# Attention with a top-1 mixture of experts: a reordered start, two steps of VectorE moved, and the experts' tokens turned by half-row transposes

## The chip, the cores and the metric

The kernel runs on one core of a Trainium2 chip. The metric is the device time of one execution in microseconds. The engines are TensorE (PE in the rows; PEld is its weight load), VectorE (DVE), ScalarE (ACT), GpSimd (POOL) and SyncE (SP). DMAs are issued from the queues of SP, ScalarE and GpSimd.

## The reference

```python
def _attn_ref(q, k, v, s):                      # (8, 8, 576, 64); s is (8, 8, 576)
    scores = scale * np.matmul(q, k.transpose(0, 1, 3, 2))
    cum = np.cumsum(np.maximum(s, 0.0), axis=-1)
    bias = -(cum[:, :, :, None] - cum[:, :, None, :])
    scores = np.where(causal, -1000000000.0, scores + np.minimum(bias, 0.0))
    attn = softmax(scores)
    return np.matmul(attn, v)

def _moe_ref(x, w_gate, w1, w2):                # x: (4608, 512), 8 experts, hidden 1024
    probs = softmax(x @ w_gate); expert_idx = argmax(probs)
    for e in range(E):
        out[mask_e] = gate_w * (np.maximum(xe @ w1[e], 0.0) @ w2[e])
```

Each token goes to the one expert with the highest logit.

## The kernel before, in words

**Attention.** The 64 heads are worked in 32 pairs, two heads on 128 partitions. For a pair, the scores of five query groups (S0 to S4) are TensorE products in fp32r; q and k are split into a high and a low part, and three products of the parts are summed. The decay bias enters as one more product: a selector `pick` times a table `cu`, built once at the start from the running sum of s. VectorE takes the row maximum while it evicts the scores (Z), ScalarE the exponentials (X), TensorE turns them by 64-row transposes (T, `half_turn`, L294), VectorE or ScalarE evicts them (C), TensorE multiplies with v (AV), and VectorE copies the output (XB). GpSimd makes the low parts of q and k for the next pairs (L215, L222).

The start (`__init__`, L77 to L174) is outside that order: VectorE clips s (L138), takes the running sum (L139), the centres (L141, L144) and the low part (L147), makes the low parts of pair 0 (`split`, L215 and L222), and then builds the table group by group (`build`, L184), after ScalarE has centred each group (`center`, L177). While nothing else is ready TensorE runs a warm-up of products of zeros (L157 to L162).

**The order.** For attention each engine has a list, written out by hand, of steps with a lag in pairs (`ORDER`, L37 to L42); `loop` emits them in turn as their needs are met. Each four pairs make a batch of tokens, whose routing (RA to RD, with CH1, CH2, CI, EX, EI, DI and SE between) is threaded through the same lists. Step 0 makes the logits, step 1 turns them and takes their maximum (`route`, L381 to L420), step 2 ranks the tokens (L421 to L445, with the operation on `base` at L439), steps 3 to 7 turn and scale the tokens (L446 to L458). `scale` (L343 to L355) takes the reciprocals of the softmax sums; SE calls it for the last batch but one. GpSimd then scatters token rows to the buffer `xs` in DRAM (L465). `HASTE` places the steps of the last batch but one by hand; the last batch is routed inside expert 0's first layer.

**Experts.** For each expert, `load_x` and `finish_x` bring 512 rows and a tail from `xs` into `xr`. The tokens must stand with their 512 features on partitions: `trans_group` (L786 to L795) turns one group of 128 features by four TensorE transposes of 128x128 into one PSUM bank of the pool `ps_x` (three banks), and `split` (L729) evicts it into a high part on ScalarE (L730) and a low part on VectorE (L731). `layer1` (L811) runs 96 products of 512 columns (L820), `layer2` (L858) 24 products for each of four token blocks (L846). The transposes for the next expert stand between those blocks (`run`, L982 to L987):

```python
for k in range(NSTAT):
    self.layer2(e, k)
    for d in ((0, 1), (2,), (3,), ())[k] if more else ():
        self.trans_group(e + 1, d)
    if more and k == (1 if e else X0[1]):
        x4 = self.trans_block(...)
```

`trans_block` turns the fifth block of rows by four more whole transposes (L800). What is left of the tokens is worked by `tails` in branches that depend on the counts.

Of the kernel before, what the change touches and what calls it, by code (L numbers as in the profile page):

```python
# [8 lines left out]
F32 = mybir.dt.float32  # L9
# [35 lines left out]
WARM = 24  # L45
# [6 lines left out]
THIN_AT = (2, 2)  # L52
X0 = (1, 2, 1)
# [23 lines left out]
class Attention:  # L77
    def __init__(self, ctx, tc, K, qkv, s, rt, ps_t):
# [39 lines left out]
        nc.gpsimd.memset(self.half, 0.0)  # L118
        for h in range(2):
            nc.gpsimd.memset(self.half[64 * h : 64 * h + 64, h], 1.0)  # L120
# [3 lines left out]
        nc.gpsimd.memset(self.mask8, 0.0)  # L124
# [4 lines left out]
        for h in range(2):  # L129
            r = slice(64 * h, 64 * h + 64)  # L130
            nc.gpsimd.affine_select(
                out=self.mask8[r, 512:], in_=self.mask8[r, 512:], pattern=[[-1, 64]],
                compare_op=ALU.is_ge, fill=BIG, base=0, channel_multiplier=1,
            )
        self.split(0, 5)
        for part in (0, 2):
            self.split(0, part)
# [19 lines left out]
        for x in range(WARM):  # L157
            for c in ((0, 256), (256, 512)) if x % 3 == 0 else ((0, 512),):
                nc.tensor.matmul(
                    warm[:, c[0] : c[1]], zb[:, :P], zb[:, P + c[0] : P + c[1]],  # L160
                    start=True, stop=True, skip_group_check=True,
                )  # L162
        nc.gpsimd.memset(self.Es[MIX][:, S:], 0.0)
        self.LT = rt.tile([P, 640], F32, name="LT", bufs=1)
        nc.gpsimd.memset(self.LT[:, S:], 0.0)
        self.xb, self.sums, self.sumx, self.rr, self.ra = [], [], [], [], []
        for i in range(2):
            self.xb.append(rt.tile([P, 4, 640], F32, name=f"xb{i}", bufs=1))
            nc.gpsimd.memset(self.xb[i][:, :, S:], 0.0)
            self.sums.append(rt.tile([P, 4, 8], F32, name=f"sums{i}", bufs=1))  # L170
            self.sumx.append(rt.tile([P, 4], F32, name=f"sumx{i}", bufs=1))
            self.rr.append(rt.tile([P, 5, 8], F32, name=f"rr{i}", bufs=1))
            nc.gpsimd.memset(self.rr[i][:, 4], 1.0)
            self.ra.append(rt.tile([P, 2, 5, 4], F32, name=f"ra{i}", bufs=1))  # L174

    def center(self, g):
        self.nc.scalar.activation(  # L177
            self.cu[:, TO[g] : TO[g] + TW[g]], self.cum[:, : TW[g]], AF.Identity,
            scale=self.sign[:, 0:1], bias=self.cen[:, 0, g : g + 1],
        )  # L180
# [25 lines left out]
    def split(self, p, part):  # L206
# [3 lines left out]
        if part == 0:  # L210
            d["q"] = self.lq.tile([P, 2, S], F32R, name="q")
            nc.scalar.activation(d["q"][:, 0], q, AF.Copy)  # L212
# [3 lines left out]
        elif part == 2:  # L216
            d["kh"] = self.ld.tile([P, S], F32R, name="kh")
            nc.scalar.activation(d["kh"], k, AF.Copy)
# [399 lines left out]
    def loop(self):  # L618
# [6 lines left out]
        self.todo = constants(self.nc, self.const, self.K, self.wg)  # L625
# [73 lines left out]
class Experts:  # L699
# [86 lines left out]
    def trans_group(self, e, d):  # L786
# [7 lines left out]
        self.split(x[:, 0, d], x[:, 1, d], t)  # L794

# [169 lines left out]
    def run(self):  # L965
        for e in range(E):
# [24 lines left out]
def constants(nc, cp, K, wg):  # L991
    blank = cp.tile([P, WIDE], F32, name="blank")[:, :ROW]
    nc.gpsimd.memset(blank[:, : DM + 1], 0.0)
    nc.gpsimd.iota(blank[:, DM + 1 :].bitcast(I32), pattern=[[0, 1]], base=1 << 20, channel_multiplier=0)
    K["blank"] = blank
    K["wg"] = cp.tile([P, 4, 32], F32, name="wg")
# [115 lines left out]
```

## Time and profile before

| | |
|---|---|
| median of the three runs shown | 785.6 us (785.55, 785.6, 787.28) |
| the profiled execution | 784.42 us, of which the span is 782.7 us |
| busy TensorE | 758.6 us (97% of the span) |
| busy VectorE, ScalarE, GpSimd | 477.2, 414.7, 219.6 us |
| attention, then experts | about 0 to 322 us, then to the end |

A row gives the start, the time taken, the engine, the line of the kernel, the operation, what it writes and reads, its shape and how many were merged; what stands in brackets is how long the engine sat idle before it, and what ended that.

### The profile page before, as it was taken

The page shows a single profiled execution, that of the slowest core. Times are in us where ns is not written, and L with a number is a line of the kernel's source. Part 1 is how long each engine was busy: PE and PEld are TensorE (multiplying, and loading weights), DVE is VectorE, ACT ScalarE, POOL GpSimd, SP SyncE. Part 2 cuts the span into 40 slices and gives each one's busy share as a digit, 9 for nine tenths or more (in the row PEclk, how much of TensorE's full clock was granted, in tenths as well). Part 3 has the DMA queues.
Part 4 walks back from the last instruction along what each step waited for, and adds up shares of the span by engine and source line. Part 5 has one row for each costly group of instructions (what it writes and reads, how often), then busy time and mean ns, then how long its engine had stood idle before and what let it go on. Part 6 is the DMA issues. An engine that isn't in the chain of part 4 may idle for free.

```text
span 782.7 us, 17835 instructions
## 1 busy us (share of the span) xinstructions
PE 758.6 (97%) x6972; PEld 624.4 (80%) x6972; DVE 477.2 (61%) x1247; ACT 414.7 (53%) x1002; POOL 219.6 (28%) x328
## 2 busy tenths in 40 slices
PE   7999999999999988999999999999999999999995
PEld 5888888888888867678788887888888888888874
DVE  7778989899999999655263544522642453633520
ACT  7998888888888866523251432412521431513410
POOL 7544455656564645321001011010011001010011
PEclk9999999999999999999999999999999999999998
DMA  7763234434343414575172642710630271720101
GB/s 263 220 217 99 96 123 131 137 116 150 103 151 107 163 53 149 189 242 201 49 249 95 212 153 87 273 44 16 218 134 28 97 259 57 255 95 22 54 29 41
DMA packets 43903, 105.24 MB, mean 134 GB/s; under 512 B 3983, under 2 KB 3983, under 8 KB 43792
## 3 DMA queue, kind: packets, MB, share of 16 engines
q1 hardware_dynamic: 35408, 80.13, 30.6%
q0 software_dynamic: 5936, 18.92, 6.5%
q10 hardware_dynamic: 2448, 4.74, 1.8%
q8 instruction: 67, 1.10, 0.6%
q14 instruction: 44, 0.36, 0.2%
HBM read 75.91 MB, written 28.12 MB: 133 GB/s over the span
## 4 chain that ended last, share of the span: by engine, by line
issue 37%; DMA 12%; PE 4%; another core or an unknown queue 4%; POOL 3%; DVE 2%; POOLq 1%; ACT 1%; DVEq 0%
DMA xs<-xr,dsi 6%; DMA out_dram<-y,xr 6%; POOL out_dram L853 2%; PE t L332 1%; PE ph L820 1%; PE s L238 1%; PE t L296 0%; DVE z L278 0%; ACT aT L322 0%; POOLq L946 0%; DVE dd L406 0%; POOLq L853 0%; DVE xb L321 0%; POOLq L1107 0%
## 5 line engine op out<-in xcount | busy, mean ns | idle before, releaser
L846 PE MATMUL py<-w2t,hT 128*128 128x512 f32 x768 | 181.3, 392 | 1.2 <-DVEq L960 1.2
L820 PE MATMUL ph<-xT,w1t 128*128 128x512 f32 x768 | 178.3, 391 | 0.6 <-PEq L949 0.6
L820 PEld LDWEIGHTS ph<-xT,w1t 128*128 128x128 f32 x768 | 143.2, 188 | 31.9 <-issue 2.3
L292 ACT ACTIVATE E<-z,m 128x128 f32<-128x128 f32 (+4 forms) x288 | 165.8, 580 | 3.1 <-DVE m L278 3.1
L846 PEld LDWEIGHTS py<-w2t,hT 128*128 128x128 f32 x768 | 142.6, 188 | 30.4 <-issue 1.5
L853 POOL DMA_INDIRECT out_dram<-y,xr x39 | 37.9, 972 | 393.6 <-DVE y L852 331.0
L278 DVE CUSTOM_DVE_ANT_0 z<-s,mask 128x128 f32<-128x128 f32 (+4 forms) x288 | 139.0, 516 | 6.4 <-ACT E L292 0.6
L852 DVE TENSOR_SCALAR y<-py,xr 128x512 f32<-128x512 f32 x35 | 26.3, 751 | 117.5 <-PE py L846 117.5
L332 PE MATMUL t<-aT,v 128*64 128x64 f32 (+2 forms) x1408 | 95.2, 291 | 0.1
L822 ACT ACTIVATE hT<-ph 128x512 fp32r<-128x512 f32 x64 | 38.1, 596 | 96.4 <-PE ph L820 96.0
L332 PEld LDWEIGHTS t<-aT,v 128*64 128x64 f32 x1408 | 66.6, 137 | 18.8 <-issue 2.8
L825 DVE SCALAR_TENSOR_TENSOR hT<-ph,hT 128x512 fp32r<-128x512 f32 x64 | 44.2, 690 | 60.7 <-ACT hT L822 60.6
L238 PE MATMUL s<-kh,q 64*128 64x512 f32 (+3 forms) x512 | 80.2, 318 | 0.0
L322 ACT COPY aT<-t 128x1024 f32<-128x1024 f32 x64 | 57.5, 898 | 38.0 <-PE t L296 38.0
L238 PE MATMUL s<-cu,pick 64*128 64x128 f32 (+4 forms) x320 | 71.9, 374 | 2.5 <-DVE base L439 1.2
L296 PEld LDWEIGHTS t<-ident,E 64*128 64x128 f32 x1600 | 63.8, 138 | 9.2 <-ACT E L292 2.7
L296 PE MATMUL t<-ident,E 64*128 64x64 f32 x1600 | 67.4, 223 | 2.4 <-ACT E L292 0.9
L730 ACT ACTIVATE xT<-t 128x512 fp32r<-128x512 f32 x32 | 18.4, 597 | 90.9 <-PE t L793 90.9
L321 DVE COPY aT<-t 128x256 f32<-128x256 f32 (+2 forms) x96 | 61.6, 641 | 3.9 <-PE t L296 3.5
L292 ACT ACTIVATION_READ_ACCUMULATOR E<-z,m 128x1 f32 x288 | 55.3, 192 | 0.0
L238 PEld LDWEIGHTS s<-cu,pick 64*128 64x128 f32 (+1 forms) x320 | 36.6, 186 | 22.3 <-issue 10.1
L215 POOL TENSOR_TENSOR q<-qk,q 128x576 fp32r<-128x576 f32 x31 | 44.2, 1426 | 32.1 <-ACT q L212 32.0
(159 smaller groups left out, 1016.6 us busy)
## 6 DMA issues: line engine op xcount, KB each, us to landing
raw<-in_w_dram SPq DMA_DIRECT2D x32, 1024.0 KB, 5.8
qk<-in_qkv_dram SPq DMA_DIRECT2D x32, 576.0 KB, 3.9
v<-in_qkv_dram SPq DMA_DIRECT2D x32, 320.0 KB, 4.3
xr<-xs SPq DMA_DIRECT2D x8, 1028.0 KB, 5.7
xs<-blank ACTq DMA_DIRECT2D x9, 514.0 KB, 5.8
xs<-blank SPq DMA_DIRECT2D x8, 514.0 KB, 4.3
xr<-xs SPq DMA_DIRECT2D x8, 514.0 KB, 8.6
xs<-xr,dsi POOLq DMA_INDIRECT x40, 3.4
```

Of the source, the lines that this page charges most:

```text
L215: return e.tensor_tensor(out=d["q"][:, 1], in0=q, in1=d["q"][:, 0].bitcast(F32), op=ALU.subtract)
L238: self.nc.tensor.matmul(out, terms[n][0], terms[n][1], start=n == 0, stop=n == len(terms) - 1, skip_group_check=True)
L278: ins = nc.vector.tensor_tensor_reduce(out=cut(z[:, :w]), in0=x, in1=mask, scale=-0.125, scalar=3.0e38, op0=ALU.add, op1=ALU.min, accum_out=m,
L292: nc.scalar.activation(out, z[:, :w], AF.Exp, bias=m, scale=-1.0, accum_out=total)
L296: self.nc.tensor.transpose(out, src[r], self.K["ident"][r, r])
L321: return self.nc.vector.tensor_copy(o, i)
L322: return self.nc.scalar.copy(o, i)
L332: nc.tensor.matmul(ps[64 * h : 64 * h + 64, bank, lo - 512 * bank : hi - 512 * bank], v[:, kt, h], self.aT[p % 2][:, kt, h, lo:hi], start= ...
L820: nc.tensor.matmul(ps, w[:, a, d, c], x[:, b, d], start=n == 0, stop=n == 11)
L825: nc.vector.scalar_tensor_tensor(out=h[:, 1, f], in0=ps, scalar=0.0, in1=h[:, 0, f].bitcast(F32), op0=ALU.max, op1=ALU.subtract)
L846: self.nc.tensor.matmul(ps, hT[:, a, f, c], w[:, b, f % 4], start=f == 0 and i == 0, stop=f == 7 and i == 2)
L853: disjoint(self.tc, "out", self.nc.gpsimd.indirect_dma_start(out=self.out, out_offset=IndirectOffsetOnAxis(ap=row[:, DM + 1 : DM + 2].bitc ...
```

## The change

At the start: s comes in two loads of 64 rows, on two queues, instead of four of 32; q and k of pair 0 come as two loads on the same two queues; the first centre and the first build go ahead of the splits of pair 0; the `half` memsets and the selector of pair 0 go ahead on GpSimd, and the memsets of `mask8`, of the fifth score tile's pad and of `blank` wait for VectorE's last split of pair 0; the pads of the logits and of the output buffers move into the generator of constants, whose steps VectorE's CO calls, so that the later constants and the load of the gate weights come one pair later. The warm-up has 12 rounds of four products with 128 columns and 6 of one with 512, instead of 24 rounds of 512 columns in one or two products. In VectorE's order SE moves from the end of a round (lag 3) to behind RDd (lag 4, so to the next round), and CI from behind RCd to ahead of Z2. The tokens of experts 1 to 7 are turned by transposes of 64 rows, in two runs of sixteen (two groups of 128 features, four token blocks, two row halves that lie in two PSUM banks), one behind layer 2's first block and one behind its third. The kernel's text in short:

```diff
-    "DVE": "RAd+4 RDd+4 C4+3 ... RBd+3 Z2+2 RCd+3 CI+3 C1+2 XB+3 Z0+1 CO+1 SE+3",
+    "DVE": "RAd+4 RDd+4 SE+4 C4+3 ... RBd+3 CI+3 Z2+2 RCd+3 C1+2 XB+3 Z0+1 CO+1",
-WARM = 24
+WARM = 18
+PAIR_AT = (0, 2)
...
+        nc.gpsimd.memset(self.half, 0.0)
+        for h in range(2):
+            nc.gpsimd.memset(self.half[64 * h : 64 * h + 64, h], 1.0)
         s4 = s.rearrange("(p h) c -> h p c", h=2)
-        for x in range(4):
-            nc.sync.dma_start(raw[32 * x : 32 * x + 32], s4[x // 2])
-        self.load(0)
+        x = self.ldx.tile([P, 2 * S], F32, name="qk")
+        for i, queue in enumerate((nc.sync, nc.scalar)):
+            queue.dma_start(raw[64 * i : 64 * i + 64], s4[i].unsqueeze(0).broadcast_to([2, 32, S]))
+        for i, queue in enumerate((nc.sync, nc.scalar)):
+            queue.dma_start(x[:, S * i : S * i + S], self.qkv[0][:, S * i : S * i + S])
+        self.st[0] = dict(x=x)
+        self.split(0, 5)
...
-        self.split(0, 5)
-        for part in (0, 2):
-            self.split(0, part)
...
-        for g in ORD:
+        self.center(ORD[0])
+        for part in (0, 2):
+            keep(self.split(0, part))
+        for g in ORD[1:]:
             self.center(g)
         keep(nc.vector.tensor_scalar(out=low, ...))
+        self.build(ORD[0])
         for part in (1, 3):
-            keep(self.split(0, part))
-        self.build(ORD[0])
+            ins = self.split(0, part)
+            keep(ins)
+        self.begun = getattr(ins, "ins", ins).name
+        after(tc, nc.gpsimd.memset(self.mask8, 0.0), [self.begun])
...
         for x in range(WARM):
-            for c in ((0, 256), (256, 512)) if x % 3 == 0 else ((0, 512),):
+            w = P if x < 12 else 512
+            for c in range(0, 512, w):
                 nc.tensor.matmul(
-                    warm[:, c[0] : c[1]], zb[:, :P], zb[:, P + c[0] : P + c[1]],
+                    warm[:, c : c + w], zb[:, :P], zb[:, P + c : P + c + w], start=True, stop=True, skip_group_check=True
...
+    def blanks(self):
+        nc = self.nc
+        rest = constants(self.tc, self.const, self.K, self.wg, self.begun)
+        yield next(rest)
+        nc.gpsimd.memset(self.LT[:, S:], 0.0)
+        for i in range(2):
+            nc.gpsimd.memset(self.xb[i][:, :, S:], 0.0)
+            nc.gpsimd.memset(self.rr[i][:, 4], 1.0)
+        yield
+        yield from rest
...
+    def trans_pair(self, e, i):
+        xr = self.X[e][0]
+        if i == 0:
+            self.X[e][1] = self.xt.tile([P, 2, 4, 512], F32R, name="xT")
+        x = self.X[e][1]
+        ts = [self.turned() for a in range(2)]
+        for d in range(2):
+            for k in range(NSTAT):
+                for a in range(2):
+                    r = slice(HP * a, HP * a + HP)
+                    o = HP * (NSTAT * d + k)
+                    c = P * (2 * i + d)
+                    self.nc.tensor.transpose(ts[a][:, o : o + HP], xr[r, k, c : c + P], self.K["ident"][r, r])
+        for a in range(2):
+            hi, lo = (
+                x[:, b, 2 * i : 2 * i + 2].rearrange("p d (k a c) -> p a d k c", k=NSTAT, a=2)[:, a] for b in range(2)
+            )
+            self.split(hi, lo, ts[a].rearrange("p (d k c) -> p d k c", d=2, k=NSTAT))
...
-                for d in ((0, 1), (2,), (3,), ())[k] if more else ():
-                    self.trans_group(e + 1, d)
+                if more and k in PAIR_AT:
+                    self.trans_pair(e + 1, PAIR_AT.index(k))
```

## Rows read from the trace of the kernel before

**Rows 1.** Busy time by stretch: PE, PEld, DVE, ACT, POOL, then granted clock, DMA share, GB/s

```profile
0.00:20.00 20.00, 15.75 (x143) 10.77 (x145) 15.96 (x43) 14.54 (x33) 15.58 (x49) 1.00 0.76 265
...
100.00:200.00 100.00, 100.00 (x1613) 84.02 (x1610) 90.94 (x302) 85.91 (x239) 56.09 (x81) 1.00 0.41 136
...
700.00:750.00 50.00, 49.88 (x234) 40.77 (x232) 20.25 (x33) 18.07 (x34) 2.87 (x3) 1.00 0.11 36
```

**Rows 2.** Timeline of the start up to the first scores, from several engines

```profile
0.82 1.79 SPq L109 DMA_DIRECT2D aT<-in_s_dram  x4
...
4.32 0.46 DVE L138 TENSOR_SCALAR aT<-aT 128x576 f32<-128x576 f32 x1 [1.75 <-DMA aT<-in_s_dram]
...
4.91 1.46 POOL L231 TENSOR_TENSOR pick<-sel,half 128x128 fp32r<-128x128 f32 x1
...
6.50 0.68 ACT L212 ACTIVATE q<-qk 128x576 fp32r<-128x576 f32 x1 [3.67 <-DMA qk<-in_qkv_dram]
...
8.56 1.56 DVE L184 SCALAR_TENSOR_TENSOR cu<-aT,cen,cu 128x128 fp32r<-128x128 f32 x3
...
9.09 0.33 PE L238 MATMUL s<-cu,pick 64*128 64x128 f32 x2 [0.18 <-POOL pick L230]
```

**Rows 3.** Timeline near 12 us: a build on VectorE beside a split on GpSimd

```profile
11.93 1.41 POOL L215 TENSOR_TENSOR q<-qk,q 128x576 fp32r<-128x576 f32 x1 [1.16 <-ACT q L212]
...
11.99 1.76 DVE L184 SCALAR_TENSOR_TENSOR cu<-aT,cen,cu 128x384 fp32r<-128x384 f32 x1
```

**Rows 4.** Timeline of the warm-up: its products, and its last 19 weight loads

```profile
1.60 7.31 PE L159 MATMUL s<-aT 128*128 128x256 bf16 x32 [1.60 <-DVE aT L103]
...
5.42 3.00 PEld L159 LDWEIGHTS <-aT 128*128 128x128 bf16 x19 [0.28 <-issue]
```

**Rows 5.** Timeline of the scale step of batch 6 and what waits for it

```profile
280.64 1.41 POOL L215 TENSOR_TENSOR q<-qk,q 128x576 fp32r<-128x576 f32 x1
...
281.07 1.01 DVE L351 TENSOR_SCALAR rr<-sums 128x32 f32<-128x32 f32 x1
...
284.25 0.16 DVE L439 TENSOR_TENSOR base<-base,s 128x8 f32<-128x8 f32 x1
...
284.56 0.38 PE L238 MATMUL s<-cu,pick 64*128 64x256 f32 x2 [1.22 <-DVE base L439]
```

**Rows 6.** Timeline of the logits' maximum of batch 6; last, all eight of L406 (min/median/max)

```profile
291.56 0.32 DVE L397 TENSOR_TENSOR both<-part 128x160 f32<-128x160 f32 x1
...
292.25 1.44 POOL L215 TENSOR_TENSOR q<-qk,q 128x576 fp32r<-128x576 f32 x1
...
292.62 2.50 DVE L406 TENSOR_TENSOR dd<-L,mx 128x40 f32<-128x40 f32 x1
...
293.62 1.42 POOL L222 TENSOR_TENSOR kl<-qk,kh 128x576 fp32r<-128x576 f32 x1
...
296.85 0.46 PE L296 MATMUL s<-ident,xb 64*128 64x64 f32 x8 [2.39 <-DVE m L278]
...
L406 DVE TENSOR_TENSOR dd<-L,mx x8: 190/200/2497, 78.7 to 333.3; 128x40 f32<-128x40 f32 x8
```

**Rows 7.** Timeline of PE: products around eight whole transposes, and a layer of 96

```profile
412.19 0.62 PE L846 MATMUL py<-w2t,hT 128*128 128x512 f32 x2
...
413.75 0.63 PE L846 MATMUL py<-w2t,hT 128*128 128x512 f32 x2
...
431.56 22.02 PE L820 MATMUL ph<-xT,w1t 128*128 128x512 f32 x96 [0.15 <-PEq L949]
```

**Rows 8.** Timeline of PE and PEld: products around sixteen half transposes of the routing

```profile
336.97 0.40 PE L820 MATMUL ph<-xT,w1t 128*128 128x512 f32 x1
...
337.30 0.57 PEld L296 LDWEIGHTS t<-ident,xb 64*128 64x128 f32 x16 [0.37 <-DVE num L1064]
...
338.29 0.39 PE L820 MATMUL ph<-xT,w1t 128*128 128x512 f32 x1
```

**Rows 9.** Groups by line and shape: weight loads of half transposes

```profile
L296 PEld LDWEIGHTS t<-ident,E 64*128 64x128 f32 x1600 | 63.8, 138 | 9.2 <-ACT E L292 2.7 <-issue 1.3 <-ACT aT L322 0.4
```

More of the change, by code (lines that the diff above doesn't have):

```diff
@@ L117, in __init__ @@
             nc.gpsimd.memset(sign[32 * x : 32 * x + 32, 1:2], 8.0 * (x % 2))
-        nc.gpsimd.memset(self.half, 0.0)
-        for h in range(2):
-            nc.gpsimd.memset(self.half[64 * h : 64 * h + 64, h], 1.0)
         self.mask = cp.tile([P, 640], F32, name="mask")
@@ L128, in __init__ @@
         )
[L129 to L134, printed above, removed]
-        self.split(0, 5)
-        for part in (0, 2):
-            self.split(0, part)
         keep(nc.vector.tensor_scalar(out=raw, in0=raw, scalar1=0.0, scalar2=None, op0=ALU.max))
@@ L144, in __init__ @@
         keep(nc.vector.tensor_scalar(out=self.cen[:, 1], in0=mid, scalar1=sign[:, 1:2], scalar2=None, op0=ALU.mult))
-        for g in ORD:
+        self.center(ORD[0])
+        for part in (0, 2):
+            keep(self.split(0, part))
+        for g in ORD[1:]:
             self.center(g)
         keep(nc.vector.tensor_scalar(out=low, in0=cum, scalar1=sign[:, 1:2], scalar2=None, op0=ALU.mult))
+        self.build(ORD[0])
         for part in (1, 3):
-            keep(self.split(0, part))
-        self.build(ORD[0])
+            ins = self.split(0, part)
+            keep(ins)
+        self.begun = getattr(ins, "ins", ins).name
+        after(tc, nc.gpsimd.memset(self.mask8, 0.0), [self.begun])
+        for h in range(2):
+            r = slice(64 * h, 64 * h + 64)
+            nc.gpsimd.affine_select(
+                out=self.mask8[r, 512:], in_=self.mask8[r, 512:], pattern=[[-1, 64]],
+                compare_op=ALU.is_ge, fill=BIG, base=0, channel_multiplier=1,
+            )
         self.build(ORD[1])
@@ L157, in __init__ @@
         for x in range(WARM):
-            for c in ((0, 256), (256, 512)) if x % 3 == 0 else ((0, 512),):
+            w = P if x < 12 else 512
+            for c in range(0, 512, w):
                 nc.tensor.matmul(
-                    warm[:, c[0] : c[1]], zb[:, :P], zb[:, P + c[0] : P + c[1]],
-                    start=True, stop=True, skip_group_check=True,
+                    warm[:, c : c + w], zb[:, :P], zb[:, P + c : P + c + w], start=True, stop=True, skip_group_check=True
                 )
-        nc.gpsimd.memset(self.Es[MIX][:, S:], 0.0)
+        after(tc, nc.gpsimd.memset(self.Es[MIX][:, S:], 0.0), [self.begun])
         self.LT = rt.tile([P, 640], F32, name="LT", bufs=1)
-        nc.gpsimd.memset(self.LT[:, S:], 0.0)
         self.xb, self.sums, self.sumx, self.rr, self.ra = [], [], [], [], []
@@ L624, in loop @@
         self.plan()
[L625 removed]
+        self.todo = self.blanks()
         self.unbuilt = list(ORD[3:])
@@ L989, in run, with constants @@
                 self.tails(e, x4)
-def constants(nc, cp, K, wg):
+def constants(tc, cp, K, wg, begun):
+    nc = tc.nc
     blank = cp.tile([P, WIDE], F32, name="blank")[:, :ROW]
-    nc.gpsimd.memset(blank[:, : DM + 1], 0.0)
+    after(tc, nc.gpsimd.memset(blank[:, : DM + 1], 0.0), [begun])
     nc.gpsimd.iota(blank[:, DM + 1 :].bitcast(I32), pattern=[[0, 1]], base=1 << 20, channel_multiplier=0)
     K["blank"] = blank
+    yield
     K["wg"] = cp.tile([P, 4, 32], F32, name="wg")
```

13 lines of the change are left out of this document (6 added, 7 removed), and 2 rows, old and new, of the table ORDER.

## The prediction

> **What bounds the kernel now.** I read the busy time by stretch first, because one share for the whole span would hide the stages. From 100 to 200 us TensorE is busy all the time, and from 700 to 750 us it idles 0.12 us [rows 1]: attention in its steady state and the experts are both bound by TensorE. The granted clock is 1.00 in these stretches and in the first 20 us, the 2.4 GHz level [rows 1]. So time is to be had in two ways only: fewer TensorE nanoseconds in the experts, or fewer holes where TensorE is not yet bound (the first 20 us) or is held up (280 to 300 us, at the end of attention). Then the timeline of those two stretches: at the start one chain of VectorE, fed by loads and by ScalarE, leads to the first scores at 9.09 us [rows 2]; at the end two waits of TensorE stand out, 1.22 us and 2.39 us, both released by VectorE [rows 5, 6]. Last the timeline of TensorE around the transposes, to price a run of them as it lies between long products [rows 7, 8].
>
> **Part 1, the start.** VectorE idles until the four loads of the gate input s have landed, at 4.32 us; their four issues on SP take 1.79 us [rows 2], 0.45 us each, and the last one decides. Now two issues on two queues do it, each with 64 rows, so the last starts 1.3 us earlier; I count 1.0 us, because a load is twice as large. From there the chain runs without a gap: clip, running sum, centres, low part, two splits of q and k, first build, first scores [rows 2]. In the new order the first centre and the first build go ahead of the splits, which shortens nothing in sum (VectorE does the same work ahead of the second build), but the splits must not become late: ScalarE's split of q waited for qk until 6.50 [rows 2]. qk is now issued in two halves right behind s, on both queues, about 1.2 us earlier, so it comes earlier by as much as the chain does. The mask memsets, the two pads and the blank go behind the start of the splits on GpSimd; they are about 2.5 us of its time, hidden by its waits for ScalarE's q (1.16 us at 11.93 [rows 3]); if that cover were gone, GpSimd's split for pair 1 would hold the scores of pair 1 back. I take a gain of 1.0 us. Bounds: nothing, if GpSimd's pick product (1.46 us in the trace [rows 2]) now falls before the signs that the centres read; and 2.2 us, if also the build of 1.76 us is no longer held by the GpSimd split that starts 0.06 us before it [rows 3] (three builds ahead of it took 1.56 us together [rows 2], so up to 1.2 us is in that); the two could as well start in the other order, but nothing in the trace says so.
>
> **Part 2, the warm-up.** 9216 columns instead of 12288, 48 of the 54 products with 128. In the trace the products run at half pace until about 5.4 us, though the granted clock reads 1.00 there too: 13 of 32 are out by then, in 3.8 us, and the other 19, 7424 columns, take 3.5 us [rows 4]. So 128 columns cost about 0.105 us before that point and half of that after it: 36 small products to 5.4 us, 12 more in 0.7 us, and six of 512 in 1.4 us: the end is near 7.5 us, where it was 8.91, and the last split is then due at about 7.9. It costs nothing, hidden by the chain of part 1; if the chain gained more than 1.5 us, the warm-up would be next.
>
> **Part 3, the turn to the experts.** Two steps of VectorE's hand-written order move. Scale of batch 6 (SE) now stands behind the rank step instead of ahead of it. In the trace its small operations start at 281.07 and drag, the first for 1.01 us, beside the GpSimd split that began at 280.64; only at 284.25 comes the base operation that frees the score bank, and TensorE waits 1.22 us for it [rows 5]. With the two rank operations first, base is done near 281.5, before TensorE asks. The drag stays, as GpSimd sets its end, but VectorE's next eviction starts 0.3 us sooner and the row maximum behind it need not wait another 0.3 us for its scores: by VectorE, which is late next, 0.65 us remain of the 1.22. The second: the logits' maximum (CI) goes ahead of a pair of row maxima and one scaled block. In the trace its last operation, 128x40 elements, takes 2.50 us: it begins at 292.62, after a GpSimd split began, and ends when the next one ends (293.62 plus 1.42); the median of its eight is 0.2 us. Behind it queue an eviction, the output copy and the row maximum for which TensorE waits 2.39 us [rows 6]. Moved ahead, the four operations end 1.2 us after the logits, near 291.2, before the GpSimd split that starts at 292.25. What they push back: the pair of row maxima by 1.2 us, which frees a score bank that TensorE asks for only after its products with v, and ScalarE's exponentials, which stand behind the late operation anyway. VectorE then reaches the row maximum after the scores of pair 31 with TensorE some 0.5 us ahead: about 1.8 us of the 2.39 are gained. Both together 2.45 us; bounds 0.65 (the second gains nothing) and 3.6 (both waits vanish).
>
> **Part 4, the transposes of experts 1 to 7.** Each expert had 16 whole transposes, and now 32 of half the rows, in two runs of 16. What a run costs is what it adds between long products. One product of 512 columns takes 0.228 us (22.02 us for 96). Two products before a run of 8 whole transposes start at 412.19, the second product behind it at 413.75: 1.56 less three products is 0.877 us, 0.110 each [rows 7]. For halves the route steps inside expert 0's first layer show the same form: last product before at 336.97, second product behind at 338.29: 1.32 less two products is 0.865 us for 16 halves [rows 8]. The 16 weight loads themselves fill 0.57 us, so that 0.3 us of each run are entry and exit: the loads begin 0.10 us after the product before has streamed, and the product behind comes late. Per expert: 16 x 0.110 = 1.75 us before, 2 x 0.865 = 1.73 after, 0.02 us gained, 0.15 us over seven. The evictions stay 4 and 4 of 512 elements per expert, written in pieces of 64; they lie beside the next 24 products (5.5 us) and cost nothing; two banks at once of three are free there. Bounds: a gain of 0.3 us per run if entry and exit vanished (4.1 us more in all), a loss as in the fourth rival. The nearest row is the run itself, so I take 0.15.
> The Trainium skill speaks on both sides here. TensorEngine Tiling (Array Packing), Theoretical Speedup, gives up to 2x for a small dimension of 64; by that, as an estimate, this part would be 6.1 us instead of 0.15 (half of 1.75, seven times); rival (a) is its case. Its Key Properties say that changing the tiling mode drains the engine; the 0.3 us of [rows 8] agree with that one.
>
> **Sum.** 1.0 + 2.45 + 0.15 = 3.6 us off the profiled execution's 784.42, which lies 0.15% under the median of the runs, 785.6. As a median: 782.0. Nothing behind 300 us gives it back: TensorE is bound again from there, the waits for loads that the trace shows there are ScalarE's and not TensorE's, and the tail of the last store is as before.
>
> **Rivals.** (a) The drain is hidden in this place and halves run as fast as their loads: two runs of about 0.57 us [rows 8], 0.6 us less per expert, 4.1 us more: 777.9. For it: loads fill their run without a hole. Against: [rows 8]. (b) The second move of part 3 puts a new wait in place of the one removed: the row maxima 1.2 us later hold the exponentials, and TensorE its transposes, for as long; of part 3 only 0.65 stays: 783.8, within 0.3%. For it: VectorE and ScalarE are both near full in attention (91 and 86 of 100 us [rows 1]). (c) The start gains nothing, as k now comes over ScalarE's queue and GpSimd works behind: 783.0. (d) Slower: the two row halves don't run side by side. One weight load of a half takes 138 ns [rows 9]; one after the other, 32 of them are 4.4 us where 1.75 stood, plus 0.6 of entry and exit: 3.3 us x 7 = 23 us, 805. It decides from about 62 ns for a half, entry and exit apart (0.84 us more per expert: 2.4 us and the 3.45 of the other parts, over seven). Against it: 16 loads in 0.57 us [rows 8]. The Trainium skill's TensorE: Matmul & The Clock Gate (LDWEIGHTS) gives a load the same time whatever its rows; the 138 ns agree, and taken alone it would speak for (d). (e) The change doesn't do what it says at the start: with small products the clock still stands at 1.2 GHz at the first scores. TensorE's 15.75 us of work up to 20 us [rows 1], less the warm-up's 7.31 [rows 4], would take up to twice that, of which waits hide half: 4 us lost and 1.0 not gained: 787.
>
> **How the numbers follow.** The three runs shown lie 0.22% apart, so 0.3%, 2.4 us, is about what a measurement can tell from no change. Forecast 0.56, (a) 0.12, (b) 0.16, (c) 0.09, (d) 0.03, (e) 0.04. Faster: 0.56 less a twentieth for its own slow end, (a) and (c), which lies 2.6 us under the median: 0.74. Same: (b) and that twentieth: 0.19. Slower: (d) and (e): 0.07. The range takes in the forecast, (b) and (c), and half the way to (a), by part 1's upper bound too: 778.8 to 784.4.
>
> **What would show it.** First scores at about 8 us; the base operation before 282 and no wait of 1.2 us behind it; the 128x40 operation at 0.2 us and TensorE's 2.39 us wait under 0.6; a run of 16 halves between products at 0.87 us and an expert's period, product to product, unchanged within 0.1 us. Wrong would be: periods shorter by 0.5 us or more, which is (a), a new VectorE wait between 290 and 300 us, which is (b), or first scores at 9 us or later.

## The result, and the profile after

The changed kernel takes 792.05 us (median; 791.25 to 792.75, four runs) against 785.95 us: a ratio of 1.0078 [1.0061, 1.0096]. It is slower by 0.8%, where 3.6 us less were forecast. The profiled execution took 792.75 us, with a span of 791.0 us. Medians leave out two executions far slower than the others of their kernel: one of 804.92 us of the kernel before, on the third chip used below, and one of 1482.04 us of the version with 65 warm-up products.

The first thing to read is where the two traces part. This table gives the start of the same product in each (us), and the distance to the kernel before:

| TensorE begins | before | after | distance |
|---|---|---|---|
| first scores | 9.09 | 17.31 | +8.2 |
| first product with v | 23.63 | 33.41 | +9.8 |
| a product with v late in attention | 276.58 | 286.51 | +9.9 |
| the same, next batch (SE lies between) | 290.63 | 299.06 | +8.4 |
| the same, one more (CI lies between) | 304.18 | 310.68 | +6.5 |
| expert 1, first layer | 385.44 | 391.47 | +6.0 |
| expert 7, first layer | 715.23 | 723.34 | +8.1 |
| span | 782.7 | 791.0 | +8.3 |

So nearly 10 us are lost ahead of the first product with v, the two moved steps give back 3.4 us of them, and 2 us are lost again among the experts. The timeline of the start of the changed kernel, which answers to [rows 2] and [rows 4]:

```profile
0.81 0.74 SPq L114 DMA_DIRECT2D aT<-in_s_dram  x1
0.81 1.45 ACTq L114 DMA_DIRECT2D aT<-in_s_dram  x1
...
1.60 7.01 PE L167 MATMUL s<-aT 128*128 128x128 bf16 x54 [1.60 <-DVE aT L104]
...
13.95 0.46 DVE L133 TENSOR_SCALAR aT<-aT 128x576 f32<-128x576 f32 x1 [12.05 <-DMA aT<-in_s_dram]
...
16.17 0.49 ACT L192 ACTIVATE cu<-aT,cen,sign 128x128 fp32r<-128x128 f32 x1 [11.46 <-DVE cen L136]
...
17.31 0.47 PE L253 MATMUL s<-cu,pick 64*128 64x128 f32 x2 [8.71 <-DVE cu L199]
```

VectorE's clip of s starts at 13.95 us instead of 4.32: it waits 12.05 us for a load that was issued at 0.81. Both issues are over by 2.3 us, so it is the transfer itself that is long. What a transfer lacks is seen in the DMA view of the first 20 us of the same kernel (40 slices of half a microsecond; the first line is the mean busy share of the 16 DMA engines in tenths, the last two give KB each):

```profile
DMA  0000037899999999999999831111138899821105
GB/s 0 0 0 0 9 88 152 237 287 296 284 286 313 286 249 295 263 257 276 326 328 291 260 113 57 48 55 46 55 68 141 345 400 403 183 72 51 44 16 132
...
aT<-in_s_dram SPq DMA_DIRECT2D x1, 144.0 KB
aT<-in_s_dram ACTq DMA_DIRECT2D x1, 144.0 KB
```

From 12 to 14.5 us the digits are 1, at some 50 GB/s: most of the sixteen engines have nothing left to do, and some two of them (a tenth to two tenths of sixteen) still carry the loads of s. Total bandwidth is not what they wait for. The times at which the semaphores of the loads count up, which the trace holds too, say the same. The first load of s in the kernel before counts up in sixteen steps, from 2.46 to 2.75 us. Each of the two wide loads has one step soon after its issue and two late ones: at 9.17 and 9.97 us on SP's queue, at 13.27 and 13.92 on ScalarE's. VectorE starts 0.03 us after the last of them.

The late start costs a second time. The busy time by stretch (TensorE, its weight loads, VectorE, ScalarE, GpSimd, then granted clock, DMA share, GB/s) of the changed kernel:

```profile
5.00:10.00 5.00, 3.60 (x24) 2.32 (x22) 0.00 (x0) 0.00 (x0) 0.00 (x0) 1.00 1.04 283
10.00:15.00 5.00, 0.00 (x0) 0.00 (x0) 1.02 (x2) 0.00 (x0) 0.00 (x0) 0.60 0.43 132
15.00:20.00 5.00, 2.19 (x14) 1.85 (x16) 4.66 (x12) 3.83 (x7) 1.79 (x5) 0.50 0.57 179
20.00:25.00 5.00, 5.00 (x28) 3.86 (x26) 3.84 (x15) 4.78 (x15) 4.73 (x9) 0.53 0.33 108
```

TensorE is idle from 8.6 to 17.3 us, the granted clock falls to 0.50 (1.2 GHz) in that idle time, and nearly all scores up to 25 us are computed at that level. That is the step from +8.2 to +9.8 in the table; with the loads cut (below), which keeps the clock at 1.00, the same two rows lie 1.24 and 1.21 us ahead, without such a step. In the kernel before the clock was 1.00 here [rows 1].

At the turn to the experts, the timeline of VectorE in the changed kernel answers to [rows 5]:

```profile
290.88 0.16 DVE L454 TENSOR_TENSOR base<-base,s 128x8 f32<-128x8 f32 x1
290.96 0.61 DVE L366 TENSOR_SCALAR rr<-sums 128x32 f32<-128x32 f32 x1
291.49 1.46 DVE L366 TENSOR_SCALAR rr<-sumx 64x4 f32<-64x4 f32 x2
```

The view of one source line answers to the last row of [rows 6] (ns, min/median/max):

```profile
L421 DVE TENSOR_TENSOR dd<-L,mx x8: 190/200/202, 88.7 to 339.8; 128x40 f32<-128x40 f32 x8
```

The base operation comes ahead of the scale's small ones, which still drag (1.46 us for two), but TensorE no longer waits for them; and none of the eight 128x40 operations takes 2.50 us any more. Of TensorE's two waits the one of 1.22 us is gone, and of the 2.39 us 0.45 are left:

```profile
303.34 0.46 PE L311 MATMUL s<-ident,xb 64*128 64x64 f32 x8 [0.45 <-DVE m L293]
```

### The profile page after: what moved, and what is told of

It is laid out like the page before. It is cut to its first block, busy times and chain, and to the rows that moved or that the text cites. A ratio compares the mean times of both kernels' runs of the same rounds, so it can differ in the third digit from the quotient of the medians.

```text
span 791.0 us, 18096 instructions
## 1 busy us (share of the span) xinstructions
PE 761.3 (96%) x7106; PEld 624.3 (79%) x7106; DVE 473.2 (60%) x1247; ACT 414.7 (52%) x1002; POOL 218.5 (28%) x328
## 4 chain that ended last, share of the span: by engine, by line
PE 37%; issue 37%; DMA 14%; another core or an unknown queue 4%; POOL 3%; DVE 2%; ACT 1%; POOLq 1%; ACTq 0%; DVEq 0%
PE s L253 16%; PE t L347 12%; DMA xs<-xr,dsi 6%; DMA out_dram<-y,xr 6%; PE t L311 6%; POOL out_dram L887 2%; DMA qk<-in_qkv_dram 2%; PE s L311 2%; PE ph L854 1%; PE s L390 1%; ACT E L307 1%; ACT aT L337 1%; DVE z L293 0%; DVE rr L366 0%
## 5 line engine op out<-in xcount | busy, mean ns | idle before, releaser
L253 PEld LDWEIGHTS s<-kh,q 64*128 64x128 f32 x512 | 50.2, 189 | 1.6 <-ACT kh L233 0.3
```

Of the source, the lines that this page charges most:

```text
L253: self.nc.tensor.matmul(out, terms[n][0], terms[n][1], start=n == 0, stop=n == len(terms) - 1, skip_group_check=True)
```

## Experiments

Two theories for the start were set against each other. Theory 1: the shape of the load is at fault. Each load of s is now described as 2 by 32 rows (the 2 is the repeat), and few engines carry a load whose outer count is 2. Theory 2: the queues or the new order of the loads are at fault. Twelve kernels were compared with the kernel before on the same chip; four more settled what was then open. The kernel before took 785.58 us on the chip of the first four, 791.2 to 792.0 us on the chips of the others, so times are compared as ratios on one chip. The one trace of the kernel before has the first chip's time, 784.42 us; of the sixteen runs the first four were traced there, the others on the other three chips.

**Cut loads.** The changed kernel, each 64-row load as two of 32 rows, same queue:

```diff
-            queue.dma_start(raw[64 * i : 64 * i + 64], s4[i].unsqueeze(0).broadcast_to([2, 32, S]))
+            for j in range(2):
+                queue.dma_start(raw[64 * i + 32 * j : 64 * i + 32 * j + 32], s4[i])
```

> The changed kernel, but each of the two 64-row loads of s is cut into two loads of 32 rows on the same queue, so that nothing differs but how the same bytes are cut. Theory 1 (a load whose outermost dimension is 2 is carried by two of the sixteen DMA engines only, so s lands 10 us late and all that is queued on those two engines behind it): s lands by 4 us, first scores near 8 us, granted clock 1.00 throughout, and the time is before less 1.0 (start), 3.4 (order) and 0.4 (transposes): about 781, between 780 and 782.5. Theory 2 (two queues at once hold each other up, ScalarE's above all): s still lands later than 10 us, the time stays at 791 to 793.

Measured: 781.73 us against 785.58, ratio 0.9961 [0.9948, 0.9973]. Its timeline:

```profile
3.95 0.46 DVE L134 TENSOR_SCALAR aT<-aT 128x576 f32<-128x576 f32 x1 [2.06 <-DMA aT<-in_s_dram]
...
7.85 0.33 PE L254 MATMUL s<-cu,pick 64*128 64x128 f32 x2
```

This one edit takes the 10 us away: theory 1, not the queues, and not the order. The first scores now come 1.24 us ahead of [rows 2], but the loads are not what gives that: the clip starts 0.37 us earlier (3.95 for 4.32). By the first transposes the lead is down to 0.33 us (11.96 for 12.29), and it is 1.21 us at the first product with v (22.42 for 23.63). In between stands the last build of the table, 1.76 us long beside GpSimd's split in [rows 3]; here the split begins at 12.67 us, behind it:

```profile
11.59 0.61 DVE L200 SCALAR_TENSOR_TENSOR cu<-aT,cen,cu 128x384 fp32r<-128x384 f32 x1
```

**Wide loads alone.** The kernel before, its four loads of s as two 64-row loads, both on SP:

```diff
-        for x in range(4):
-            nc.sync.dma_start(raw[32 * x : 32 * x + 32], s4[x // 2])
+        for i in range(2):
+            nc.sync.dma_start(raw[64 * i : 64 * i + 64], s4[i].unsqueeze(0).broadcast_to([2, 32, S]))
```

> The kernel before, with s in two loads of 64 rows, both on SP, in place of four of 32; nothing else. Theory 1: s lands at 8 us or later (64 packets for each of two engines), q and k behind it, first scores between 13 and 18 us, time 7 to 11 us over before, 792 to 797. Theory 2: one queue, so nothing changes: first scores at 9 us, time 785 to 787.

Measured: 798.39 us, ratio 1.0165 [1.0147, 1.0182]; more than expected. Its timeline and its stretches:

```profile
13.62 0.46 DVE L138 TENSOR_SCALAR aT<-aT 128x576 f32<-128x576 f32 x1 [11.04 <-DMA aT<-in_s_dram]
```

```profile
15.00:20.00 5.00, 0.00 (x0) 0.00 (x0) 3.99 (x7) 4.04 (x8) 2.84 (x5) 0.50 0.48 150
20.00:25.00 5.00, 4.30 (x28) 3.52 (x28) 4.73 (x13) 3.08 (x10) 2.46 (x3) 0.50 0.52 182
```

The cause alone, on one queue and in the old order, reproduces the wait, and the low clock with it. It is dearer here by some 3 us (the first product with v is 12.5 us late, for 9.8): with q and k behind the loads on the same queue, ScalarE's split of q, too, starts at 14.70 us, and the first scores at 20.26 us.

**Repeat or count?** A load of 2 by 32 rows has a small outer count and also reads each row twice. The first try to part the two described the first load of q and k as 2 by 64 rows:

```diff
-        self.nc.sync.dma_start(x, self.qkv[p][:, : 2 * S])
+        src = self.qkv[p][:, : 2 * S]
+        self.nc.sync.dma_start(x, src.rearrange("(a p) c -> a p c", a=2) if p == 0 else src)
```

> The kernel before with one edit: the first load of q and k (128 rows, 590 KB) is described as two parts of 64 rows, without any repeated source; the same bytes, the same queue, one issue. If what made the loads of s slow is that their outermost count is 2, this load becomes slow too: with s in two parts 295 KB took some 11 us, so 590 KB take 20 us or more, ScalarE's split of q starts behind 20 us where it started at 6.50, and the time is 12 us or more over the kernel before. If it was that each source row was read twice, the split starts at 6.5 us as before and the time is the same.

It tested nothing: the two halves lie one behind the other in memory, and the built program holds the load merged into 128 rows, as before (790.71 us, the kernel before beside it 791.23). So its trace shows the kernel before on the second chip. With `"(p a) c -> a p c"` in the same place, even rows and then odd rows, it can't be merged, and a = 16 is the control (the first pair then has its rows in another order, so these two kernels don't compute the reference):

> The kernel before with one edit: the first load of q and k (128 rows, 590 KB, SP's queue) reads its rows in another order, all even ones and then all odd ones, so that the source is described as 2 by 64 rows and cannot be merged into one row count; each row is read once, and the bytes are the same. It changes the values of the first pair. If a count of 2 on the outside of a load is what makes it slow, ScalarE's split of q, which started at 6.50 us in the kernel before, starts behind 20 us, since 295 KB of s in two such parts took some 11 us. If it was the reading of each row twice, it starts at 6.5 us as before.

> The same edit with 16 by 8 rows (each sixteenth row together), again every row once and the same bytes; it changes the values of the first pair. If the count on the outside decides, 16 is as good as 128: ScalarE's split of q starts at 6.5 us within 0.5. If any order of rows that cannot be merged makes a load slow, it starts as late as with 2 by 64.

ScalarE's split of q, which stands at 6.50 in [rows 2], with a = 2 and with a = 16 (802.32 and 793.08 us, one run each, beside 791.4):

```profile
18.26 0.68 ACT L213 ACTIVATE q<-qk 128x576 fp32r<-128x576 f32 x1 [15.43 <-DMA qk<-in_qkv_dram]
```

```profile
7.73 0.68 ACT L213 ACTIVATE q<-qk 128x576 fp32r<-128x576 f32 x1 [4.89 <-DMA qk<-in_qkv_dram]
```

Each row is read once in both, and the bytes are the same: an outer count of 2 delays the load by 11.8 us, one of 16 by 1.2 (more than the half microsecond allowed). The count decides, not the repeat. The Trainium skill's page DMA: Bandwidth & Descriptors, section Why a DMA increments its semaphore by 16 and not by 1, has the rule: a transfer is spread over the largest number of engines up to 16 that divides the slowest dimension of both sides. By it the changed loads get two engines; the digit 1 in the DMA view agrees, and so do the semaphores: two late steps for each wide load of s and for this load with a = 2 (18.03 and 18.24 us), sixteen steps with a = 16 (7.04 to 7.71 us).

**The two moved steps alone.** The kernel before with only VectorE's new order:

```diff
-    "DVE": "RAd+4 RDd+4 C4+3 Z1+2 Z3+2 C0+2 Z4+2 SC+4 DI+4 CH2+4 CH1+4 RBd+3 Z2+2 RCd+3 CI+3 C1+2 XB+3 Z0+1 CO+1 SE+3",
+    "DVE": "RAd+4 RDd+4 SE+4 C4+3 Z1+2 Z3+2 C0+2 Z4+2 SC+4 DI+4 CH2+4 CH1+4 RBd+3 CI+3 Z2+2 RCd+3 C1+2 XB+3 Z0+1 CO+1",
```

> The kernel before with SE and CI moved in VectorE's order, nothing else. Theory: both waits of TensorE go, as in the changed kernel, where the distance to before fell by 1.5 us over the scale step and by 1.9 us over the logits' maximum: 3.4 us faster, 782.3 to 783.0. Rival: a part of that came from the later start (another phase of GpSimd against VectorE): only the predicted 2.45 or less, 783.5 or more.

Measured: 780.83 us, ratio 0.9945 [0.993, 0.9959]. By the ratio that is 4.3 us and by the medians 4.75, more than expected. Its trace shows less than that: against the kernel before, the product with v is 1.3 us earlier behind SE (289.30 for 290.63) and 3.25 behind CI (300.93 for 304.18); the spans differ by 3.9 (778.8 for 782.7), as expert 0 lacks a hole of 0.61 us that the kernel before has. For the rest, another run with the kernel before's order gives a hint.

**The half transposes alone.** The kernel before with the transposes of experts 1 to 7 in row halves:

```diff
-                for d in ((0, 1), (2,), (3,), ())[k] if more else ():
-                    self.trans_group(e + 1, d)
+                if more and k in PAIR_AT:
+                    self.trans_pair(e + 1, PAIR_AT.index(k))
```

> The kernel before with the tokens of experts 1 to 7 turned by half-row transposes, nothing else. Theory (entry and exit of a run cost what the halves save): between 0 and 0.6 us faster in all, a run of 16 between products at 0.87 us. Rival (a): 4 us faster. Rival (d) and its kin: slower by 1 us or more; the changed kernel's distance grew by 0.8 us at one tail and 1.7 us at one layer, and if the new transposes cause that, it shows here again at the same places.

Measured: 784.03 us, ratio 0.998 [0.9969, 0.999]. Its stretches around the end of attention, which it shares with the kernel before, and below them those of the run with the moved steps alone:

```profile
295.00:300.00 5.00, 2.91 (x48) 2.67 (x50) 4.80 (x14) 3.34 (x11) 3.70 (x6) 0.87 0.68 235
300.00:305.00 5.00, 4.53 (x51) 3.79 (x47) 3.31 (x14) 3.95 (x11) 0.00 (x0) 0.79 0.31 109
```

```profile
295.00:300.00 5.00, 4.54 (x63) 3.81 (x59) 4.69 (x18) 5.00 (x15) 2.47 (x3) 1.00 0.92 333
300.00:305.00 5.00, 4.46 (x82) 3.61 (x84) 4.06 (x17) 1.53 (x6) 2.91 (x3) 1.00 0.29 112
```

Behind TensorE's 2.39 us wait the granted clock can fall to 1.2 GHz. Here it did, and the distance to the kernel before's trace grew from 0.25 to 1.74 us across that place. In the profiled execution of before it happened not to. Among the 21 runs of the kernel before beside it the two with the highest mean clock (0.997) took 783.9 us and the two with the lowest (0.991, 0.992) 786.2 and 786.8; the five runs with the moved steps all have 0.996 or 0.997. So on this chip removing the wait also removes the chance of low clock behind it; that this is what is missing is likely, not shown.

On the three other chips it is otherwise, against what was expected of the runs there: in all seven traces that have the moved steps VectorE holds TensorE anew, for 1.4 to 2.2 us at 298 to 300 us, and between 300 and 315 us the clock falls to 0.50 to 0.69 of a stretch. What holds VectorE there no view names. One of them, with 32 warm-up products (below):

```profile
299.82 0.45 PE L254 MATMUL s<-cu,pick 64*128 64x384 f32 x2 [2.17 <-DVE m L294]
...
300.00:305.00 5.00, 4.41 (x51) 3.73 (x52) 4.75 (x21) 2.88 (x9) 1.54 (x2) 0.52 0.08 32
```

As to the transposes: before and after, one second layer of 96 products (first row of each, and the first product of the layer behind it, which stands at 431.56 in [rows 7]):

```profile
407.20 5.61 PE L846 MATMUL py<-w2t,hT 128*128 128x512 f32 x24
412.64 1.04 PE L793 MATMUL t<-ident,xr 128*128 128x128 f32 x8
413.43 5.72 PE L846 MATMUL py<-w2t,hT 128*128 128x512 f32 x24
```

```profile
413.23 5.60 PE L880 MATMUL py<-w2t,hT 128*128 128x512 f32 x24
418.76 0.71 PE L823 MATMUL t<-ident,xr 64*128 64x64 f32 x16
419.41 5.75 PE L880 MATMUL py<-w2t,hT 128*128 128x512 f32 x24
...
437.55 2.75 PE L854 MATMUL ph<-xT,w1t 128*128 128x512 f32 x11
```

The layer takes 24.36 us before (431.56 less 407.20) and 24.32 after (437.55 less 413.23): 0.04 us for this expert. A run of 16 halves holds TensorE 0.65 us where 8 whole ones held it 0.79, but it starts later: product to product over it is 6.18 us (419.41 less 413.23), over the whole ones 6.23 (413.43 less 407.20). The growth of 0.8 and 1.7 us that the changed kernel shows at one tail and at one layer is not there in the run with the transposes alone (-0.04 and +0.17 us), so they don't cause it.

**The start and the steps in pairs.** What the parts are worth together, on one other chip:

> The kernel before with the new start alone (order of the loads, splits, builds and memsets, and the warm-up with small products), but each 64-row load of s cut into two loads of 32 rows; VectorE's order and the transposes as before. Theory 1 (the parts add up): first scores near 7.9 us, attention 1.1 us ahead of the kernel before as in the run with the cut loads, the 2.39 us wait for the row maximum near 296 us still there, and the median 1.1 us under the kernel before (some 784.4 against 785.5). Theory 2 (the new start is worth nothing by the end, its 1.1 us come back as holes with no releaser in TensorE's expert stage): median within 0.5 us of the kernel before, with over 1 us of such holes behind 310 us.

> The changed kernel with the loads of s cut into 32 rows and with the whole transposes of the kernel before. If the parts add up, 1.1 us (start) and 4.7 us (the two moved steps, as run alone by medians) off 785.5: 779.7, and the granted clock of the runs 0.996 to 0.997. If the half-row transposes are worth the 1.5 us by which they alone were faster, this is 1.5 us slower than the run with the cut loads: 783.2. If the new start's gain comes back in the expert stage, the same as the moved steps alone: 780.8.

> The kernel before with the two moved steps and the half-row transposes, and the old start. If the half-row transposes are worth 0.03 us an expert, as their periods in the run alone show: 780.6, the same as the moved steps alone (780.8). If they are worth 1.5 us: 779.3. In either case no low clock behind 290 us, since the 2.39 us wait ahead of it is gone.

| kernel, with the cut loads | median us | ratio to before |
|---|---|---|
| new start alone | 791.45 | 1.0009 [0.9995, 1.0023] |
| new start and moved steps | 788.87 | 0.9972 [0.9958, 0.9987] |
| old start, moved steps and half transposes | 787.07 | 0.9948 [0.9934, 0.9961] |

The parts don't add up. In their traces the new start is 1.1 us ahead all through attention, as it should be, and yet worth nothing at the end, as theory 2 had it. With the moved steps it comes out later than any case named for it, and the granted clock of those runs is 0.990 to 0.995 where 0.996 to 0.997 was expected. The half transposes add nothing to the moved steps that these ratios show (0.9948; alone, on the first chip, 0.9945). Something behind 310 us takes the start's gain away: on this chip a product with v stands at 312.83 us with the new start and the moved steps and at 318.68 in the program of the kernel before (the merged load), 5.9 us apart, and the spans, 786.9 and 789.0, are 2.1 us apart. TensorE's waits from 320 us on (total us, times, longest) show it for the changed kernel, then for the kernel before:

```profile
PE ph L854 <- issue: 1.4, 1, 1.4
PE py L880 <- DVEq L994: 1.3, 1, 1.3
PE ph L942 <- issue: 1.0, 2, 0.6
```

```profile
PE py L846 <- DVEq L960: 1.2, 1, 1.2
PE ph L820 <- PEq L949: 0.6, 3, 0.3
PE ph L908 <- issue: 0.6, 1, 0.6
```

"Issue" is idle time without a releaser. It is 2.4 us for 0.6, once 1.39 us in the middle of a layer where nothing is late:

```profile
666.07 1.61 PE L854 MATMUL ph<-xT,w1t 128*128 128x512 f32 x6
669.07 2.11 PE L854 MATMUL ph<-xT,w1t 128*128 128x512 f32 x8 [1.39 <-issue]
```

Theory 3 was that the 22 more warm-up products shift the whole of TensorE's code, and that its position decides where such holes fall.

**The warm-up alone,** in the kernel before:

```diff
-WARM = 24
+WARM = 18
...
-            for c in ((0, 256), (256, 512)) if x % 3 == 0 else ((0, 512),):
+            w = P if x < 12 else 512
+            for c in range(0, 512, w):
```

> The kernel before with the new warm-up alone: 54 products, 48 of them with 128 columns, 9216 columns. The first scores do not move (9.1 us, TensorE is ready from 7.6 us on), and the granted clock stays 1.00 up to 10 us. Theory 3: some 2 us of holes with no releaser behind 310 us where the kernel before has 0.6 (on the chip of the first runs) and a time 1 to 2 us over the kernel before. Rival: the same time within 0.5 us.

Measured: 793.36 us, ratio 1.004 [1.002, 1.006]. Its runs lie between 792.15 and 798.1 us, and the medians are 1.9 us apart, 0.2%. Attention runs as before (within 0.15 us of the first chip's trace, up to 280 us), the clock is 1.00 up to 10 us. The waits from 320 us on are shown here; the second answers to the 1.2 us of the kernel before, whose program has 0.7 us of "issue" in its trace from the second chip.

```profile
PE ph L908 <- issue: 2.0, 3, 1.7
PE py L846 <- PEq L960: 1.8, 1, 1.8
```

**32 products in the changed kernel,** with the cut loads:

```diff
-WARM = 18
+WARM = 17
...
-            w = P if x < 12 else 512
+            w = P if x < 5 else 512
```

> The changed kernel with the cut loads of s and a warm-up of 32 products (20 of 128 columns, 12 of 512) in place of 54, so that the warm-up has as many instructions as in the kernel before; its 8704 columns end near 7.2 us, ahead of the first scores at 7.9. Theory 3 (the new start loses its 1.1 us and about 1 us more in the expert stage because 22 more products ahead of everything shift TensorE's code against the blocks in which it is fetched): holes with no releaser behind 310 us fall from 1.9 us to under 0.8, and the ratio to the kernel before is 0.993 (the moved steps' 0.9945 and 1.1 us). Rival (the loss has to do with the moved loads, memsets and blanks, or is chance): holes of about 2 us as before, ratio 0.996 as with the cut loads alone.

Measured: 784.37 us against 791.4, ratio 0.9917 [0.9904, 0.993], with 0.5 us of such holes. As it was another chip than that of the cut loads, four counts were then run on one chip, the same edit with other numbers:

> The changed kernel with the cut loads of s and its own warm-up of 54 products, beside the three that follow on one chip. Theory 3 (where TensorE's code lies sets the holes): ratio to the kernel before 0.996, with 2 us or more of holes with no releaser behind 310 us. Rival (it was the chip): the same time as with 32 products, within 0.1%.

> The same with 32 products (20 of 128 columns, 12 of 512; 8704 columns). Theory 3: ratio 0.992 to 0.993, 3 us under the kernel with 54 products, and under 1 us of such holes behind 310 us. Rival: the same as with 54.

> The same with 43 products (36 of 128 columns, 7 of 512; 8192 columns). Theory 3 says only that the holes change with the count, not in which direction: anywhere from 0.992 to 0.997. If instead more small products cost as such, it lies midway, 0.994. If only chance decides, the four agree within 0.1%.

> The same with 65 products (64 of 128 columns, 1 of 512; 8704 columns). Theory 3: anywhere from 0.992 to 0.998; if it is no later than with 54 products, the count as such is not the cost. If more small products cost as such: 0.998, 1.5 us over the kernel with 54. If only chance decides, the four agree within 0.1%.

| products | median us | ratio to before (792.01) | holes "issue" from 320 us on, us |
|---|---|---|---|
| 32 | 786.02 | 0.9923 [0.9906, 0.994] | 0.9 |
| 43 | 786.59 | 0.9931 [0.9913, 0.9948] | 3.5 |
| 54 | 788.84 | 0.9959 [0.9945, 0.9972] | 3.8 |
| 65 | 786.2 | 0.993 [0.9912, 0.9948] | 2.4 |

The waits of 54 and of 32:

```profile
PE ph L855 <- issue: 2.3, 2, 1.7
PE ph L943 <- issue: 1.5, 2, 0.9
```

```profile
PE ph L855 <- issue: 0.6, 1, 0.6
PE ph L943 <- issue: 0.3, 1, 0.3
```

It was not the chip: 54 products cost 2.8 us over 32 on one chip. Nor is it the price of more small products: 65 are as good as 43. Only 54 stands apart; 32, 43 and 65 lie within 0.6 us, about the scatter of their runs. The columns of the warm-up differ too (8192 to 9216), but that is over by the first product with v, which stands at 22.35 to 22.51 us in all four. So it is the number of instructions ahead that changes where TensorE stalls hundreds of microseconds later.

What fills most of the holes can be read from the traces. Among the DMA packets are single ones of 16 KB of the kind "instruction", on queue q8, mostly 3 to 30 us apart. In the traces of this case 23 holes without a releaser stand behind 370 us and last over 0.25 us, and each of them ends 1.3 to 1.6 us after such a packet has ended. The longest of 54 products with the line of this queue in the DMA view of 663 to 666 us, and below it the same layer with 32:

```profile
665.90 2.37 PE L855 MATMUL ph<-xT,w1t 128*128 128x512 f32 x9 [1.68 <-issue]
...
q8 instruction: 1, 0.02, 2.8%
```

```profile
661.25 7.08 PE L855 MATMUL ph<-xT,w1t 128*128 128x512 f32 x30 [0.21 <-PEq L984]
```

In both the packet starts 0.5 us behind the layer's first product (663.10 for 662.60, 661.74 for 661.25) and takes 1.3 us. With 54 products TensorE has six more products to run and then stands still until 665.90; with 32 it runs on without a break. So these holes are very likely waits for code, and what lies ahead of the code decides where they fall, as theory 3 had it; no run moved such a packet by itself. The holes at 341 to 344 us are of another kind: no such packet ended within 10 us before them, and what ends them stays open. They are 0.6, 1.5, 0.6 and 1.6 us with 32, 43, 54 and 65 products; the others come to 0.3, 2.0, 3.2 and 0.8 us, which is the order of the medians (the traced run of 43 took 788.19 us, more than its median). The version with 32 products has the lowest ratio of all (0.9917 and 0.9923) and beats both kernels; its interval overlaps with those of 43, of 65 and of the moved steps alone.

## Why the prediction was wrong

**Part 1, the start, is the step that failed,** in the words "I count 1.0 us, because a load is twice as large". The issue time, the chain and the queues were weighed; how a load of that shape is spread over the DMA engines was not, and "as large" was taken to be all that matters. In its place: two engines for each load, so that the later one lands at 13.92 us, and then 1.6 us of low clock, +9.8 in all. Its worst end was taken to be that it "gains nothing", so no bound and no rival held a late load. With the loads cut, the step's own number came out, first scores at 7.85 (about 8 was said) and 1.1 us ahead through attention (1.0 was said), but by luck: the loads moved the clip by 0.37 us, and 0.9 us of the lead come from the build that GpSimd no longer holds, which the prediction had in its upper bound alone.

**Part 2, the warm-up at no cost: wrong too,** but not where it was looked for. It ends at 8.61 us (at 7.92 with the cut loads), not near 7.5; with the cut loads the first scores wait for it, their table being ready at 7.17. By the first product with v nothing of that is left, so at the start it is hidden, as said. Its price, 0.2% alone by the medians, appears among the experts.

**Part 3, the moved steps: mechanism right on the first chip, size under-rated.** The base operation at once and no wait behind it, the 128x40 operation at 0.2 us, the 2.39 us wait under 0.6: all three came. The second move brought the 1.8 us forecast (1.9). The first brought 1.2 to 1.8 instead of 0.65: VectorE was not late next. By the traces that is 3.1 to 3.7 us instead of 2.45, about the upper bound, and by the ratio 4.3, likely since the waits also carried a chance of low clock, which the single profiled execution of before did not show. Rival (b), a new wait in its place, did not come on this chip. On the other three its sign stands in every trace with the moved steps, 1.4 to 2.2 us on VectorE, and yet these steps have the same ratio there (0.9948 with the half transposes), as the program of the kernel before loses time there too.

**Part 4, the transposes: right in size.** 0.04 us measured for one expert, 0.02 forecast. Rival (a) would have shown 0.6 less. Of the two rules weighed there (the Trainium skill, TensorEngine Tiling (Array Packing), Theoretical Speedup and Key Properties), the trace bears out the drain and not the doubled speed: sixteen halves hold TensorE 0.14 us less than eight whole ones and give 0.09 of it back at their ends. That this edit alone measured 1.5 us by medians is, by its trace, mostly not the transposes themselves: in it expert 0 is 0.8 us shorter (61.48 us from first layer to first layer, for 62.31), where the kernel before has its one hole of 0.61 us, and such holes move with the code. Rival (d), 23 us, is excluded by the same rows.

**Rival (e)** named the symptom, 1.2 GHz at the first scores, and 787 us, but the wrong cause: with the loads cut, the same 54 small products leave the clock at 1.00. It fell in the 8.7 us in which TensorE had nothing to do.

The sum by measured terms, in the traces: +9.9 start, -3.4 moved steps, +1.8 between there and the end (the holes: 2.4 us for 0.6): +8.3, the difference of the spans. The remedy costs a few lines: with the loads cut and 32 warm-up products the change is worth 0.8% in place of losing 0.8%.

## What to carry to other kernels

Before merging loads, read the description of the merged one from the outside: an issue takes 0.45 us of its queue [rows 2], but an outer count of 2 put two loads of 144 KB on two engines each, so that they landed at 9.97 and 13.92 us. A wait of TensorE costs its length and perhaps the clock behind it, so compare medians with the clock of each run before one trace is believed. When parts measured alone don't add up, look for idle time without a releaser far behind the edit, look in the DMA view for a packet of instructions just ahead of its end, and test it by changing the number of instructions ahead.

## What was unexpected in the hardware

- An outer count of 2 delays a 576 KB load by 11.8 us, one of 16 by 1.2, with the same rows read once.
- 54 products in the first 8 us in place of 32 move the end of the program by 2.8 us, 43 and 65 by 0.6 or less, and with them stalls of up to 1.7 us appear hundreds of microseconds later.
- Behind 370 us each such stall of over 0.25 us ends 1.3 to 1.6 us after a packet of 16 KB of instructions has landed, 23 of 23.
- The kernel before itself takes 785.6 us on one chip and 791.2 to 792.0 on three others. Traces of several kernels on the others show stalls of TensorE without a releaser between 306 and 312 us that the first chip's traces don't show.
